# Opening of a fused attention and GEGLU kernel: x and wk loaded in halves, fewer zero matmuls, x transposed in the logits' banks, K chunks side by side, beta and gate_w late

## The chip, the cores and the metric

The kernel runs on one core of a Trainium2 chip. The metric is the device time of one execution in microseconds (us). Five engines work side by side, each with its own instruction queue: TensorE (PE, matmuls; its weight loads are shown as PEld), VectorE (DVE), ScalarE (ACT), GpSimd (POOL) and SyncE (SP, which issues most DMAs). Each takes its instructions in order; where one needs another's result, it waits on a semaphore, and everything behind it on that engine waits too.

## The reference, cut to what matters

x is 2048 rows of 512; the attention has 32 heads of 16 and works in 4 segments of 512 rows, with a memory M, z carried from one to the next; beside it stands a gated feed-forward of width 1792.

```python
g = sigmoid((x * gate_w).sum(-1, keepdims=True))
# A: per segment s
p = softmax(q_s k_s^T * 16**-0.5 + mask);  a_dot = p v_s
a_mem = (phi(q_s) M) / (phi(q_s) z + 1e-6)
o = sigmoid(beta) * a_mem + (1 - sigmoid(beta)) * a_dot
M += phi(k_s)^T v_s;  z += sum(phi(k_s))        # then o @ wo
# B
b = (gelu(x @ w_gate) * (x @ w_up)) @ w_down
return g * a + (1 - g) * b
```

## The kernel before

All tensors live in SBUF for the whole run. x is held transposed (xT, 512 features as 4 blocks `fc` of 128 partitions, 2048 columns), since every projection contracts over features. The weights wq, wk, wv, wga (gate), wup, wdn, wo are loaded whole. G[0..2] hold the feed-forward's activations of a segment; G[1] is lent at the start to the first segment of x (x0) and a block of zeros.

The work is written in program order by hand (a manual schedule), in two parts.

**The opening** is a fixed list:

- `load_inputs` (L118): SP issues in this order x0 (L125), wk, wq, beta, wv, wga (all L120 through `cols`, beta L128), the DMA transpose of x's segment 1 (L123), gate_w (L132), wup, the transposes of segments 2 and 3, wdn, wo.
- `warm_up` (L143): DVE clears the zeros, PE runs 9 matmuls of 128x512 on them.
- `transpose_x0` (L149): for each of the 4 blocks fc, PE transposes 4 tiles of x0 into a bank T of the pool `gen`, and DVE (fc 0, 2, L156) or ACT (fc 1, 3, L158) copies the bank to xT. Each fc has its own bank.
- `setup_consts` (L160): masks, by POOL, and two small reductions on DVE.
- K of segment 0 (`u_k`, L290): three of the four chunks of 128 columns, one after another; each is 4 matmuls (one per fc) into a bank of `gen`, then DVE evicts it to ktb (L299) and multiplies it by two masks into KT (L301). Then four chunks of Q (`u_q`, L239 matmul, L244 eviction by DVE), four row tiles of V (`u_v`, L316, L320), `setup_beta` (L174: ACT's Exp of beta, then three small DVE operations to gh and og), and 14 gate chunks (`u_gate`, L360) that ACT evicts with its Gelu (L366). After the fourth of these DVE takes four absolute maxima (L185).

**The rest** is planned at build time. Streams (K, Q, V, G, U, D, O and so on) hold units of work with costs and due times; a loop over 4 segments, 4 column chunks and 5 groups A to E puts the logits of a group (L519) on PE, their Exp on ACT (L525), the masking on POOL, and fills PE with units of the streams until the Exp should be done. One unit's matmuls go into a bank of `gen` and DVE evicts it; a gate chunk of a later segment is evicted by a copy (L368) and an up chunk by a product (L387).

PSUM has 8 banks: 4 are the logits tile `lg` (pool `plg`, one buffer), 1 is `od`, and `gen` has 3. A matmul that opens a `gen` bank waits until its last user's eviction is done.

Of the kernel before, what the change touches and what calls it, by code (L numbers as in the profile page):

```python
# [13 lines left out]
P = 128  # L14
D = 512
H = 32
# [3 lines left out]
FC = D // P  # L20
NC8 = H // 8
HS = DFF // P
EXP_LIMIT = 80.0
NG = 3
NK = 3
BF = dt.bfloat16
# [18 lines left out]
def kernel(  # L45
# [15 lines left out]
    nc = tc.nc  # L61
    S = A_x.shape[1]
    L = S // NSEG
    KT = L // P
    assert A_x.shape[0] == 1 and A_x.shape[2] == D and L == 512 and KT == 4
    x2 = A_x[0]
# [5 lines left out]
    plg = ctx.enter_context(tc.tile_pool(name="plg", bufs=1, space=bass.MemoryType.PSUM))  # L72
    pod = ctx.enter_context(tc.tile_pool(name="pod", bufs=1, space=bass.MemoryType.PSUM))
    pgen = ctx.enter_context(tc.tile_pool(name="pgen", bufs=3, space=bass.MemoryType.PSUM))

    def const(shape, dtype, name):
        return cpool.tile(shape, dtype, name=name, tag=name)

    xT = const([P, FC, S], BF, "xT")
    wq = const([P, FC, D], BF, "wq")  # L80
    wk = const([P, FC, D], BF, "wk")
    wv = const([P, FC, D], BF, "wv")
    wo = const([P, FC, D], BF, "wo")
    wup = const([P, FC, DFF], BF, "wup")
# [3 lines left out]
    ident = const([P, P], BF, "ident")  # L88
    bm = const([P, 8, 17], BF, "bm")
    eo = const([P, 2], F32, "eo")  # L90
    beta = const([P, H], BF, "beta")
# [8 lines left out]
    phk = const([P, NC8, L], BF, "phk")  # L100
    G = [const([P, HS, L], BF, f"G{i}") for i in range(NG)]
    QT = const([P, NC8, L], BF, "QT")
# [12 lines left out]
    def gen(name):  # L115
        return pgen.tile([P, 512], F32, name=name, tag="gen")

    def load_inputs():  # L118
        def cols(dst, src):
            nc.sync.dma_start(dst[:, :, :], src.rearrange("(fc p) n -> p fc n", p=P))  # L120

        def x_seg(s):
            nc.sync.dma_start_transpose(xT[:, :, s * L:(s + 1) * L], x2[s * L:(s + 1) * L, :])  # L123

        nc.sync.dma_start(x0, x2[0:L, :].rearrange("(k p) d -> p k d", p=P))  # L125
        cols(wk, A_wk)
        cols(wq, A_wq)
        nc.sync.dma_start(beta[:, :], A_beta.rearrange("(o n) -> o n", o=1).to_broadcast((P, H)))  # L128
        cols(wv, A_wv)
        cols(wga, B_w_gate)  # L130
        x_seg(1)
        nc.sync.dma_start(gw[:, :], gate_w.rearrange("(fc p) -> p fc", p=P))  # L132
        cols(wup, B_w_up)
        x_seg(2)
        x_seg(3)
        cols(wdn, B_w_down)
        cols(wo, A_wo)


    x0 = G[1][:, 0:KT, :]  # L140
    zero = G[1][:, KT, :]

    def warm_up():  # L143
        nc.vector.memset(zero, 0.0)
        T = gen("warm")
        for i in range(9):
            nc.tensor.matmul(T[:, :], lhsT=zero[:, 0:P], rhs=zero, start=True, stop=True)

    def transpose_x0():  # L149
        for fc in range(FC):  # L150
            T = pgen.tile([P, 1024], BF, name="x0T", tag="gen")
            for kt in range(KT):
                nc.tensor.transpose(T[:, kt * P:(kt + 1) * P],
                                    x0[:, kt, fc * P:(fc + 1) * P], ident[:, :])
            if fc % 2 == 0:
                nc.vector.tensor_copy(xT[:, fc, 0:L], T[:, 0:512])  # L156
            else:
                nc.scalar.copy(xT[:, fc, 0:L], T[:, 0:512])  # L158

    def setup_consts():  # L160
        nc.gpsimd.memset(bm[:, :, :], 1.0)
# [12 lines left out]
    def setup_beta():  # L174
        eb = wk2.tile([P, H], F32, name="eb", tag="eb")
        nc.scalar.activation(eb[:, :], beta[:, :], AF.Exp, scale=-1.0)
        nc.vector.tensor_scalar_add(eb[:, :], eb[:, :], 1.0)
        nc.vector.reciprocal(gh[:, :], eb[:, :])
        nc.vector.tensor_scalar(out=og[:, :], in0=gh[:, :], scalar1=-1.0, scalar2=1.0,
                                op0=ALU.mult, op1=ALU.add)  # L180
# [3 lines left out]
    def absmax(i, src):  # L184
        nc.vector.tensor_reduce(out=amax[:, i:i + 1], in_=src, axis=mybir.AxisListType.XY,  # L185
                                op=ALU.max, apply_absolute_value=True)
# [10 lines left out]
    def u_bound():  # L197
# [8 lines left out]
        def spread():  # L206
            room_for_bank()
            T = gen("bT")
            for i in range(3):
# [7 lines left out]
        def test():  # L217
# [4 lines left out]
            nc.vector.tensor_scalar(out=safe[:, :], in0=bound[:, 5:6],  # L222
                                    scalar1=float(DH ** 0.5 * D * D), scalar2=EXP_LIMIT,
                                    op0=ALU.mult, op1=ALU.is_le)
# [65 lines left out]
    def u_k(s, c):  # L290
        def f():
            T = gen("kT")
            for fc in range(FC):
                nc.tensor.matmul(T[:, :], lhsT=wk[:, fc, c * P:(c + 1) * P],  # L294
                                 rhs=xT[:, fc, s * L:(s + 1) * L],
                                 start=(fc == 0), stop=(fc == FC - 1))
                if fc < FC - 1:
                    yield MM512
            nc.vector.tensor_copy(ktb[:, c, :], T[:, :])  # L299
            for p in range(2):  # L300
                nc.vector.tensor_scalar(out=KTm[p][:, (NC8 * s + c) % NK, :], in0=ktb[:, c, :],  # L301
                                        scalar1=eo[:, p:p + 1], scalar2=None, op0=ALU.mult)
            return MM512
        return 4 * MM512, EVAC + 0.6, f
# [7 lines left out]
    def u_v(s, kt):  # L312
        def f():
            T = gen("vT")
            for fc in range(FC):
                nc.tensor.matmul(T[:, :], lhsT=xT[:, fc, s * L + kt * P:s * L + (kt + 1) * P],  # L316
                                 rhs=wv[:, fc, :], start=(fc == 0), stop=(fc == FC - 1))
                if fc < FC - 1:
                    yield MM512
            nc.vector.tensor_copy(V[s % 2][:, kt, :, 0:16],  # L320
                                  T[:, :].rearrange("p (h d) -> p h d", h=H))
            return MM512
        return 4 * MM512, EVAC, f
# [32 lines left out]
    def u_gate(s, hs, direct):  # L356
        def f():
            T = gen("gT")
            for fc in range(FC):
                nc.tensor.matmul(T[:, :], lhsT=wga[:, fc, hs * P:(hs + 1) * P],  # L360
                                 rhs=xT[:, fc, s * L:(s + 1) * L],
                                 start=(fc == 0), stop=(fc == FC - 1))
                if fc < FC - 1:
                    yield MM512
            if direct:
                nc.scalar.activation(G[s % NG][:, hs, :], T[:, :], AF.Gelu_apprx_tanh)  # L366
            else:
                nc.vector.tensor_copy(G[s % NG][:, hs, :], T[:, :])  # L368
            return MM512
        return 4 * MM512, EVAC, f  # L370

    def gelu(s):
        for h0 in range(0, HS, 7):
            g = G[s % NG][:, h0:h0 + 7, :]
            nc.scalar.activation(g, g, AF.Gelu_apprx_tanh)  # L375

    def u_up(s, hs):
        def f():
            T = gen("uT")
            for fc in range(FC):  # L380
# [3 lines left out]
                if fc < FC - 1:  # L384
                    yield MM512
            g = G[s % NG][:, hs, :]
            nc.vector.tensor_tensor(out=g, in0=T[:, :], in1=g, op=ALU.mult)  # L387
# [5 lines left out]
    def u_down(s, qt):  # L393
        def f():
            T = gen("dT")
            for hs in range(HS):
                nc.tensor.matmul(T[:, :], lhsT=G[s % NG][:, hs, qt * P:(qt + 1) * P],  # L397
                                 rhs=wdn[:, hs, :], start=(hs == 0), stop=(hs == HS - 1))
# [175 lines left out]

    ctx.enter_context(tc.manual_schedule())
    load_inputs()
    make_identity(nc, ident[:, :])
    warm_up()
    transpose_x0()
    setup_consts()  # L580

# [38 lines left out]
    def room_for_bank():  # L620


        if current:
            current[0][3][0] += 1
            while current and current[0][3][0] > 2:
                step()
# [37 lines left out]
    def run(u):  # L664
        if u[0] == 0.0:
            u[2]()
        else:
            for _ in u[2]():
                pass

    for c in range(NK):
        run(u_k(0, c))
    for c in range(NC8):
        run(u_q(0, c))
    for kt in range(KT):
        run(u_v(0, kt))
    setup_beta()
    done["k", 0], done["q", 0], done["v", 0] = NK, NC8, KT
    for hs in range(HS):
        run(u_gate(0, hs, True))  # L680
        if hs == 3:
            absmax(1, wq[:, :, :])
            absmax(2, wk[:, :, :])
            absmax(0, xT[:, :, 0:L])
        if hs == HS - 3:
            absmax(3, xT[:, :, L:2 * L])
    t_act[0] = t_pe[0] + 1.9

    def u_gelu(s):
# [13 lines left out]
    for i in range(NK, NSEG * NC8):  # L703
        s, c = i // NC8, i % NC8
# [8 lines left out]
    for i in range(NC8, NSEG * NC8):  # L713
        s, c = i // NC8, i % NC8
# [99 lines left out]
    for s in range(NSEG):  # L814
        oT = wk2.tile([P, FC, L], BF, name="oT", tag="oT")
        oTs[s] = oT
        for c in range(NC8):
            for g in "ABCDE":
# [25 lines left out]
                n = 4 * NC8 * 5 - clock[0]  # L844
# [152 lines left out]
```

## Time and profile before

| what | us |
|---|---|
| median of 3 runs | 292.79 (292.26 to 293.21) |
| the profiled execution | 293.84 |
| its span, first to last instruction | 292.0 |
| PE busy | 282.9 (97%) |
| DVE busy | 215.7 (74%) |
| ACT busy | 200.7 (69%) |
| POOL busy | 82.7 (28%) |

How to read it: the page lists busy times, then the chain of waits that ended last, then groups of instructions with the idle time ahead of them and its releaser; a DMA's time is from its issue to its landing. The timeline view lists instructions by time: start, length, engine, line, operation, output and input, count, and in brackets the idle time of the engine before it and what ended it. Neighbouring instructions of one kind stand in one row, so a row's length is from the first's start to the last's end. Matmuls are pipelined: one begins before the one ahead of it has ended.

Landings of the first loads, from issue (page, last part): x0 3.9 us, wk 4.8, wq 9.0, beta 8.8, wv 9.7, wga 13.7, gate_w 3.1, wup 8.7.

### The profile page before, as it was taken

The page shows a single profiled execution, that of the slowest core. Times are in us where ns is not written, and L with a number is a line of the kernel's source. Part 1 is how long each engine was busy: PE and PEld are TensorE (multiplying, and loading weights), DVE is VectorE, ACT ScalarE, POOL GpSimd, SP SyncE. Part 2 cuts the span into 40 slices and gives each one's busy share as a digit, 9 for nine tenths or more (in the row PEclk, how much of TensorE's full clock was granted, in tenths as well). Part 3 has the DMA queues.
Part 4 walks back from the last instruction along what each step waited for, and adds up shares of the span by engine and source line. Part 5 has one row for each costly group of instructions (what it writes and reads, how often), then busy time and mean ns, then how long its engine had stood idle before and what let it go on. Part 6 is the DMA issues. An engine that isn't in the chain of part 4 may idle for free.

```text
span 292.0 us, 6916 instructions
## 1 busy us (share of the span) xinstructions
PE 282.9 (97%) x2960; PEld 138.2 (47%) x2960; DVE 215.7 (74%) x422; ACT 200.7 (69%) x125; POOL 82.7 (28%) x140
## 2 busy tenths in 40 slices
PE   7899999999999999999999999999999999999992
PEld 4344445554444454545444454455544544544451
DVE  1788488777876869987878968988768567785453
ACT  3226877768897776776898785767748968777600
POOL 4000043344204334243410424242323033244300
PEclk9999999999999999999999999999999999999998
DMA  6989940200000000400000001033101000011002
GB/s 214 325 189 251 308 84 3 54 20 2 20 0 2 20 20 18 93 20 20 18 20 18 2 2 36 3 76 34 38 0 38 2 0 20 18 21 38 22 19 79
DMA packets 29444, 15.85 MB, mean 54 GB/s; under 512 B 21984, under 2 KB 28384, under 8 KB 29408
## 3 DMA queue, kind: packets, MB, share of 16 engines
q1 hardware_dynamic: 29408, 15.35, 21.0%
q8 instruction: 25, 0.41, 0.6%
q14 instruction: 11, 0.09, 0.1%
HBM read 8.14 MB, written 2.10 MB: 35 GB/s over the span
## 4 chain that ended last, share of the span: by engine, by line
PE 56%; DVE 3%; issue 0%; DVEq 0%
PE dT L397 14%; PE uT L381 10%; PE od L546 7%; PE gT L360 6%; PE lg L519 6%; PE aT L414 4%; PE kT L294 2%; PE vT L316 2%; PE qT L239 2%; PE mn L496 1%; PE MT L434 1%; DVE ktb L299 0%; DVE G L368 0%; DVE pha L271 0%; DVE o L556 0%
## 5 line engine op out<-in xcount | busy, mean ns | idle before, releaser
L525 ACT ACTIVATE pT<-lg 128x2048 bf16<-128x2048 f32 x80 | 150.1, 1876 | 57.1 <-PE lg L519 46.0
L536 POOL TENSOR_SCALAR_AFFINE_SELECT pT<-pT 128x512 bf16<-128x512 bf16 x128 | 79.5, 639 | 194.1 <-ACT pT L525 192.2
L381 PE MATMUL uT<-xT,wup 128*128 128x512 bf16 x224 | 62.3, 379 | 0.0
L360 PE MATMUL gT<-xT,wga 128*128 128x512 bf16 x224 | 60.2, 379 | 0.6 <-DVE G L368 0.4
L397 PE MATMUL dT<-wdn,G 128*128 128x512 bf16 x224 | 55.2, 379 | 0.2 <-DVE G L387 0.2
L546 PEld LDWEIGHTS <-pT 128*128 128x128 bf16 x1280 | 43.6, 96 | 17.7 <-issue 0.4
L546 PE MATMUL od<-V,pT 128*128 128x17 bf16 x1280 | 43.9, 170 | 0.0
L387 DVE TENSOR_TENSOR G<-uT,G 128x512 bf16<-128x512 f32 x56 | 38.3, 686 | 6.8 <-PE uT L381 6.4
L368 DVE CAST G<-gT 128x512 bf16<-128x512 f32 x42 | 28.8, 685 | 8.0 <-PE gT L360 7.7
L519 PE MATMUL lg<-QT,KT 32*128 32x384 bf16 (+3 forms) x512 | 31.7, 301 | 0.0
L360 PEld LDWEIGHTS <-wga 128*128 128x128 bf16 x224 | 19.7, 97 | 22.8 <-issue 5.5
L397 PEld LDWEIGHTS <-G 128*128 128x128 bf16 x224 | 19.5, 97 | 22.2 <-issue 3.9
L381 PEld LDWEIGHTS <-wup 128*128 128x128 bf16 x224 | 19.2, 97 | 20.8 <-issue 5.0
L402 DVE TENSOR_SCALAR tB<-dT,omg 128x512 bf16<-128x512 f32 x16 | 12.0, 750 | 19.9 <-PE dT L397 19.8
L519 PEld LDWEIGHTS <-KT 32*128 32x128 bf16 x512 | 8.9, 92 | 29.8 <-issue 29.5
L375 ACT ACTIVATE G<-G 128x3584 bf16<-128x3584 bf16 x6 | 18.8, 3182 | 0.0
L239 PE MATMUL qT<-xT,wq 128*128 128x512 bf16 x64 | 17.4, 379 | 1.1 <-DMA wq<-in_A_wq_dram 1.1
L552 DVE RECIPROCAL rden<-od 128x16 f32<-128x16 f32 x32 | 8.2, 256 | 13.7 <-PE od L546 13.4
L294 PE MATMUL kT<-xT,wk 128*128 128x512 bf16 x64 | 17.1, 380 | 0.3 <-DVE xT L156 0.3
L414 PE MATMUL aT<-wo,oT 128*128 128x512 bf16 x64 | 16.4, 379 | 0.5 <-DVE G L368 0.5
L316 PE MATMUL vT<-wv,xT 128*128 128x512 bf16 x64 | 16.4, 380 | 0.0
L366 ACT ACTIVATE G<-gT 128x512 bf16<-128x512 f32 x14 | 8.4, 598 | 9.7 <-PE gT L360 9.7
(81 smaller groups left out, 226.2 us busy)
## 6 DMA issues: line engine op xcount, KB each, us to landing
out_dram<-osb SPq DMA_DIRECT2D x16, 128.0 KB, 1.7
wga<-in_B_w_gate_dram SPq DMA_DIRECT2D x1, 1792.0 KB, 13.7
wup<-in_B_w_up_dram SPq DMA_DIRECT2D x1, 1792.0 KB, 8.7
wdn<-in_B_w_down_dram SPq DMA_DIRECT2D x1, 1792.0 KB, 10.3
G<-in_A_x_dram SPq DMA_DIRECT2D x1, 512.0 KB, 3.9
wk<-in_A_wk_dram SPq DMA_DIRECT2D x1, 512.0 KB, 4.8
wq<-in_A_wq_dram SPq DMA_DIRECT2D x1, 512.0 KB, 9.0
wv<-in_A_wv_dram SPq DMA_DIRECT2D x1, 512.0 KB, 9.7
```

Of the source, the lines that this page charges most:

```text
L239: nc.tensor.matmul(T[:, :], lhsT=wq[:, fc, c * P:(c + 1) * P], rhs=xT[:, fc, s * L:(s + 1) * L], start=(fc == 0), stop=(fc == FC - 1))
L294: nc.tensor.matmul(T[:, :], lhsT=wk[:, fc, c * P:(c + 1) * P], rhs=xT[:, fc, s * L:(s + 1) * L], start=(fc == 0), stop=(fc == FC - 1))
L360: nc.tensor.matmul(T[:, :], lhsT=wga[:, fc, hs * P:(hs + 1) * P], rhs=xT[:, fc, s * L:(s + 1) * L], start=(fc == 0), stop=(fc == FC - 1))
L368: nc.vector.tensor_copy(G[s % NG][:, hs, :], T[:, :])
L381: nc.tensor.matmul(T[:, :], lhsT=wup[:, fc, hs * P:(hs + 1) * P], rhs=xT[:, fc, s * L:(s + 1) * L], start=(fc == 0), stop=(fc == FC - 1))
L387: nc.vector.tensor_tensor(out=g, in0=T[:, :], in1=g, op=ALU.mult)
L397: nc.tensor.matmul(T[:, :], lhsT=G[s % NG][:, hs, qt * P:(qt + 1) * P], rhs=wdn[:, hs, :], start=(hs == 0), stop=(hs == HS - 1))
L414: nc.tensor.matmul(T[:, :], lhsT=oT[:, fc, qt * P:(qt + 1) * P], rhs=wo[:, fc, :], start=(fc == 0), stop=(fc == FC - 1))
L519: nc.tensor.matmul(lg[:, j, off:off + n], lhsT=KTm[pp][32 * j:32 * j + 32, (NC8 * s + c) % NK, kt * P:(kt + 1) * P], rhs=QT[32 * j:32 * j ...
L525: nc.scalar.activation(pT[:, :, :], lg[:, :, :], AF.Exp, scale=DH ** -0.5)
L536: nc.gpsimd.affine_select(out=v, in_=v, pattern=pat, compare_op=ALU.is_ge, fill=0.0, base=0, channel_multiplier=-1)
L546: nc.tensor.matmul(od[:, qq, j, 0:17], lhsT=t[:, j, o:o + P], rhs=V[s % 2][:, kt, 8 * c + 2 * j + p, 0:17], start=(kt == 0), stop=(kt == qq))
```

## The change

- x0 comes in two DMAs: row tiles 2 and 3 issued by ACT, row tiles 0 and 1 by SP. wk comes in two DMAs of two fc blocks each.
- beta moves from its place behind wq, and gate_w from its place ahead of wup, to behind wup.
- 4 zero matmuls instead of 9.
- x0's transposes go into one tile of four banks from the logits' pool, first all fc blocks of row tiles 0 and 1, then those of row tiles 2 and 3; each fc block is copied when its second half is done, by the same engines as before.
- The three K chunks are begun side by side: fc 0 of all three, fc 1 of all three, then fc 2 and 3 of each with its eviction.
- `setup_beta` stands behind the 14 gate chunks instead of behind V.

```diff
-        nc.sync.dma_start(x0, x2[0:L, :].rearrange("(k p) d -> p k d", p=P))
-        cols(wk, A_wk)
+        rows = x2[0:L, :].rearrange("(k p) d -> p k d", p=P)
+        nc.scalar.dma_start(x0[:, 2:4, :], rows[:, 2:4, :])
+        nc.sync.dma_start(x0[:, 0:2, :], rows[:, 0:2, :])
+        wkr = A_wk.rearrange("(fc p) n -> p fc n", p=P)
+        nc.sync.dma_start(wk[:, 0:2, :], wkr[:, 0:2, :])
+        nc.sync.dma_start(wk[:, 2:4, :], wkr[:, 2:4, :])
         cols(wq, A_wq)
-        nc.sync.dma_start(beta[:, :], A_beta.rearrange("(o n) -> o n", o=1).to_broadcast((P, H)))
         cols(wv, A_wv)
         cols(wga, B_w_gate)
         x_seg(1)
+        cols(wup, B_w_up)
         nc.sync.dma_start(gw[:, :], gate_w.rearrange("(fc p) -> p fc", p=P))
-        cols(wup, B_w_up)
+        nc.sync.dma_start(beta[:, :], A_beta.rearrange("(o n) -> o n", o=1).to_broadcast((P, H)))
...
-        for i in range(9):
+        for i in range(ZEROS):
             nc.tensor.matmul(T[:, :], lhsT=zero[:, 0:P], rhs=zero, start=True, stop=True)
...
-        for fc in range(FC):
-            T = pgen.tile([P, 1024], BF, name="x0T", tag="gen")
-            for kt in range(KT):
-                nc.tensor.transpose(T[:, kt * P:(kt + 1) * P],
-                                    x0[:, kt, fc * P:(fc + 1) * P], ident[:, :])
-            if fc % 2 == 0:
-                nc.vector.tensor_copy(xT[:, fc, 0:L], T[:, 0:512])
-            else:
-                nc.scalar.copy(xT[:, fc, 0:L], T[:, 0:512])
+        T = plg.tile([P, FC, 1024], BF, name="x0T", tag="lg")
+        for k0 in (0, 2):
+            for fc in range(FC):
+                for kt in (k0, k0 + 1):
+                    nc.tensor.transpose(T[:, fc, kt * P:(kt + 1) * P],
+                                        x0[:, kt, fc * P:(fc + 1) * P], ident[:, :])
+                if k0 == 2 and fc % 2 == 0:
+                    nc.vector.tensor_copy(xT[:, fc, 0:L], T[:, fc, 0:L])
+                elif k0 == 2:
+                    nc.scalar.copy(xT[:, fc, 0:L], T[:, fc, 0:L])
+
+    def first_k():
+        us_ = [u_k(0, c)[2]() for c in range(NK)]
+        for _ in range(2):
+            for u in us_:
+                next(u)
+        for u in us_:
+            for _ in u:
+                pass
...
-    for c in range(NK):
-        run(u_k(0, c))
+    first_k()
     for c in range(NC8):
         run(u_q(0, c))
     for kt in range(KT):
         run(u_v(0, kt))
-    setup_beta()
...
+    setup_beta()
     t_act[0] = t_pe[0] + 1.9
```

More of the change, by code (lines that the diff above doesn't have):

```diff
@@ L23 @@
 EXP_LIMIT = 80.0
+ZEROS = 4
 NG = 3
```

## The prediction

> **What bounds the kernel now.** I read the page first: PE is busy 97% of the span, and the chain that ended last is PE work almost throughout, so whatever holds PE anywhere is paid at the end. The profiled execution took 293.84 us, a span of 292.0 us and 1.84 us around it; the median shown is 292.79. The change touches the opening and the end of the gate chunks, so next I read the timeline there (start, length, engine, line, what, count, idle time before it and its releaser).
>
> ```profile
> 0.81 1.28 ACT L158 ACT_TABLE_LOAD   x1 [0.81 <-PEq L981]
> ...
> 1.26 4.02 PE L147 MATMUL warm<-G 128*128 128x512 bf16 x9 [1.26 <-DVE G L144]
> ...
> 4.71 0.10 PEld L153 LDWEIGHTS <-G 128*128 128x128 bf16 x1 [0.34 <-DMA G<-in_A_x_dram]
> 5.07 1.69 PE L153 MATMUL x0T<-ident,G 128*128 128x128 bf16 x16
> ...
> 5.74 0.42 DVE L156 COPY xT<-x0T 128x512 bf16<-128x512 bf16 x1 [4.54 <-PE x0T L153]
> 6.17 1.21 ACT L158 COPY xT<-x0T 128x512 bf16<-128x512 bf16 x2 [4.08 <-PE x0T L153]
> ...
> 7.05 2.75 PE L294 MATMUL kT<-xT,wk 128*128 128x512 bf16 x12 [0.29 <-DVE xT L156]
> ...
> 8.11 0.69 DVE L299 CAST ktb<-kT 128x512 bf16<-128x512 f32 x1 [0.98 <-PE kT L294]
> ...
> 9.37 0.68 DVE L299 CAST ktb<-kT 128x512 bf16<-128x512 f32 x1
> ...
> 10.95 3.63 PE L239 MATMUL qT<-xT,wq 128*128 128x512 bf16 x16 [1.15 <-DMA wq<-in_A_wq_dram]
> ...
> 14.41 3.62 PE L316 MATMUL vT<-wv,xT 128*128 128x512 bf16 x16
> ```
>
> See three things. The table load of ACT lies at 0.81, under the wait for x. PE waits 0.29 us for copies and 1.15 us for wq. From 14.41, the first V matmul, PE runs without a hole: I measure the opening by when V starts.
>
> The tile view of G and wk (shortest/median/longest ns) shows the clock:
>
> ```profile
> L153 PEld LDWEIGHTS <-G x16: 98/151/151, 4.7 to 6.5; 128*128 128x128 bf16 x16
> ...
> L147 PE MATMUL warm<-G x9: 607/634/634, 1.3 to 4.6; 128*128 128x512 bf16 x9
> ```
> ```profile
> L294 PE MATMUL kT<-xT,wk x12: 376/379/379, 7.1 to 9.4; 128*128 128x512 bf16 x12
> ```
>
> A full matmul takes 634 ns before and 379 ns after some moment, and the loads 151 and 98. The zeros start 0.427 us apart (weight loads at 2.08, 2.51, 2.94), the K matmuls 0.216 us ((2.75 - 0.38) / 11), the transposes 0.107. By the tile view of short stretches the loads are of 151 ns up to 6.2 and of 98 from 6.4: PE worked about 5.1 us without a pause (from 1.26) before it ran at full speed. (The clock column says 1.00 from 0; no record lies before the first turn, so these rows carry it.)
>
> The end of the gate chunks:
>
> ```profile
> 30.77 1.28 ACT L525 ACT_TABLE_LOAD   x1
> ...
> 31.45 0.69 DVE L368 CAST G<-gT 128x512 bf16<-128x512 f32 x1 [3.23 <-PE gT L360]
> ...
> 32.06 1.88 ACT L525 ACTIVATE pT<-lg 128x2048 bf16<-128x2048 f32 x1
> 32.11 1.89 PE L360 MATMUL gT<-xT,wga 128*128 128x512 bf16 x8
> ```
>
> DVE copies the next gate chunk at 31.45 while ACT loads its table until 32.05.
>
> **The opening, step by step.** The changed kernel's instruction order holds more than the diff says. All of x0T is now one tile, and its copies and the second half's transposes wait for each other in turn: PE's transposes of fc 1 wait for DVE's copy of fc 0, those of fc 2 for ACT's copy of fc 1, those of fc 3 for DVE's copy of fc 2; ACT's first copy waits for DVE's, and ACT stands at that wait ahead of its table load, which so leaves 0.81.
>
> 1. x lands. Now its load is waited for until 4.71. The windows view has 82 GB/s in 2.0 to 2.5, 365 in 3.0 to 3.5: the start is slow, and two queues can shorten it, not the rest. Between 4.0 and 4.7; I take 4.4. Eight transposes of the first half: 0.05 + 8 x 0.107 = 0.9, so fc 0's second half starts at 5.3.
> 2. The chain. Two transposes take 0.107 + 0.314 (tile view), DVE starts 0.04 later (5.70 to 5.74) and copies 0.425: +0.89. ACT wakes (0.05), loads 1.28 and copies 0.59: +2.81. PE wakes (0.06), fc 2: 0.42, DVE 0.04 + 0.43, PE 0.06: fc 3 starts at +3.81; after its two transposes K starts at +4.02, since its first six matmuls need only fc 0 and 1, and ACT's last copy (0.59) lies under them. K starts at 9.3, not 7.05: **+2.25**. Bounds: +1.7 (x at 4.0 with 0.2 less of wakes), +2.6 (x at 4.7). Without the load in the chain it would be +0.95.
> 3. The clock. Four zeros end at about 3.0; then PE pauses for 1.4 us, works 0.9, and has only four pairs of transposes up to 9.3. Now it took 5.1 us of unbroken work. So K runs at 0.427. Its first chunk's last matmul is the eighth: 7 x 0.427 + 0.63 + 0.04, DVE starts to evict at K + 3.66. From there DVE sets the pace: 1.26 us a chunk (8.11, 9.37), the fourth Q chunk needs the bank that the first QT copy frees, 3 x 1.26 + 0.69 + 0.05 = 4.52 later, and V starts 4 x 0.216 after: K + 9.04. Now V starts 7.36 after K. **+1.7.** Bounds: at full speed from the start the eviction begins at K + 1.93 and V at K + 7.31, that is 0; slow to the end of the first Q chunk V comes at K + 9.4, +2.0. I stay near the upper end, as the row nearest to it (5.1 us) is.
>
> The Trainium skill, "TensorE: Matmul & The Clock Gate", Part 1, says that the gate opens after one busy window of some 3.4 us, and that the windows run free of the kernel's start. By it the gate could open 3.4 to 6.8 us after K starts, which leaves +1.7 to +2.0; the 5.1 us here agree.
>
> What costs nothing: the fifth to ninth zeros lay under the wait for x. wq is issued one issue (0.5 us) later, behind the second half of wk; it landed at 10.9 (1.86 + 9.0), and Q now starts at 14.4: 3.5 us of cover. This hides, too, that without beta's packets it may land earlier; the 1.15 us are thus no gain. The side by side order saves the 0.29, counted in 2. gw and beta go behind wup on SP's queue, issued by 18.7, ahead of the two x transposes: gw took 3.1 us and wup 8.7, so both are there by 28, and are needed from 32. The transposes stand behind the same number of issues as before, less beta's.
>
> **The end of the gate chunks.** beta's Exp moves behind the last gate activation and the table load, so it runs at 32.06 to 32.29 (0.23; times of now, all shifted). DVE has its three small ops ahead of the gate copy, and they wait for that Exp: the copy that stood at 31.45 waits until 32.33 + 0.69 (18.67 to 19.36 now) = 33.02. Behind it stand the up product and the next gate copies. PE has three banks: the third gate chunk after it, second half of the x8 at 32.11, starts at 32.98 and needs the bank of that copy, free at 33.02 + 0.69 + 0.05 = 33.76: **+0.78**. The bounds are 0 (a later hole takes it up) and 1.0 (if the next chunk is held as well). The 0.23 that ACT's first pT is late hides beneath: the next logits stand at 34.15 and move to 34.9, the Exp ends at 34.2.
>
> **Sum**: 2.25 + 1.7 + 0.75 = +4.7 us on a PE that has no later hole to absorb it: 298.5 for the profiled execution, which stands 1.05 above the median; the median goes to **297.5**.
>
> **Rivals.**
> - The clock turns early (short pauses count as work): K at full speed. 2.25 + 0.75: 295.8. For it: only about half of the time up to K is idle. Against: nine zeros needed 5.1 us. 14%.
> - The late beta is absorbed: 2.25 + 1.7: 296.7. For it: DVE idles 3.23 us before 31.45. Against: the Exp itself comes after that. 12%.
> - Not slower: the copies don't hold each other, and ACT's load stays at its start. Then K starts at 5.3 + 0.9 = 6.2, and with the clock turned at 6.4 as now V starts 7.31 later, at 13.5: -0.9, +0.75 of beta: 292.7. It decides if K starts before 7.0; the waits in the order speak against it. 4%.
> - The table load costs more than its row when it is waited for. Twice 1.28 on the chain: 298.8. Against: now 30.77 to 32.06 is 1.29 with nothing after it. 6%. The Trainium skill, "ScalarE: Activation LUTs", What ACT_TABLE_LOAD costs, has 1.28 us for the load and 1.38 for a drain on a switch of set; by it the sum would be 1.4 more. The row here shows no drain.
>
> Forecast 64%. The range reaches over all but the not-slower case: 295.4 (early clock, x at 4.0) to 298.9. Faster by over 0.3% 0.03, within 0.3% (0.9 us, about what a measurement of this kernel tells from no change) 0.03, slower 0.94.
>
> **What would show it.** After: ACT's table load between the first DVE copy and the first ACT copy; second-half transposes in pairs with holes; K from about 9.3 with 634 ns matmuls; V at about 18.4; DVE idle until ACT's Exp, and right behind it a PE hole of 0.8 us on a gate chunk. Wrong if K starts near 7, if K's matmuls are of 379 ns, or if V is at 14.

## The result, and the profile after

The changed kernel takes **299.25 us** (median of 6 runs, 298.92 to 299.41) against 292.94 (median of 6 runs of the kernel before, 292.26 to 293.21): ratio 1.0217, 95% interval 1.0203 to 1.0231. It is 6.3 us slower, where 4.7 were forecast. Its profiled execution took 299.41 us, a span of 297.5 and 1.91 around it.

The timeline of the changed kernel's opening (columns as in the prediction: start, length, engine, line, what, count, idle time before and its releaser; the transposes are now L160, DVE's copy L163, ACT's L165, K L311, Q L256, V L333):

```profile
4.50 1.25 PE L160 MATMUL x0T<-ident,G 128*128 128x128 bf16 x10 [1.35 <-DMA G<-in_A_x_dram]
...
5.78 0.42 DVE L163 COPY xT<-x0T 128x512 bf16<-128x512 bf16 x1 [4.58 <-PE x0T L160]
...
6.26 0.37 PE L160 MATMUL x0T<-ident,G 128*128 128x128 bf16 x2 [0.52 <-DVE xT L163]
...
6.29 1.28 ACT L165 ACT_TABLE_LOAD   x1 [6.29 <-DVE xT L163]
7.58 0.59 ACT L165 COPY xT<-x0T 128x512 bf16<-128x512 bf16 x1
8.22 0.37 PE L160 MATMUL x0T<-ident,G 128*128 128x128 bf16 x2 [1.59 <-ACT xT L165]
...
9.18 0.37 PE L160 MATMUL x0T<-ident,G 128*128 128x128 bf16 x2 [0.59 <-DVE xT L163]
...
9.35 5.08 PE L311 MATMUL kT<-xT,wk 128*128 128x512 bf16 x12
...
14.26 3.01 PE L256 MATMUL qT<-xT,wq 128*128 128x512 bf16 x12
...
17.50 1.02 PE L256 MATMUL qT<-xT,wq 128*128 128x512 bf16 x4 [0.23 <-DVE QT L261]
...
18.36 3.62 PE L333 MATMUL vT<-wv,xT 128*128 128x512 bf16 x15
```

Read the last bracket of each line as a chain. The second halves come in pairs, each after the copy of the block before, and the copies after the pairs. The table load, which stood at 0.81 before, now starts at 6.29 behind DVE's copy, and PE sits idle 1.59 us until ACT's copy is through. K starts at 9.35 instead of 7.05, and its 12 matmuls take 5.08 us instead of 2.75. V starts at 18.36 instead of 14.41.

The timeline where the gate chunks end (the late Exp is L193, DVE's three small ops L194 to L196, its gate copy L385, the gate matmuls L377):

```profile
34.71 1.28 ACT L193 ACT_TABLE_LOAD   x1
...
36.01 0.23 ACT L193 ACTIVATE eb<-beta 128x32 f32<-128x32 bf16 x1
...
36.27 0.18 DVE L194 TENSOR_SCALAR eb<-eb 128x32 f32<-128x32 f32 x1 [4.79 <-ACT eb L193]
...
36.96 0.68 DVE L385 CAST G<-gT 128x512 bf16<-128x512 f32 x1
...
37.70 1.02 PE L377 MATMUL gT<-xT,wga 128*128 128x512 bf16 x4 [0.61 <-DVE G L385]
```

DVE idles 4.79 us until the Exp that stands behind the table load, and its gate copy then holds a bank that PE wants: a hole of 0.61 us. Matched instruction by instruction, PE runs 3.95 us later than before from V on, 4.72 later from the matmul at 37.70 on, and 4.73 later at the last weight load. No later hole takes anything back.

The end of the span, in the tile view of out_dram from 280 us on, the kernel before and then the changed one (shortest/median/longest, first and last start of an issue; then the time from issue to landing):

```profile
L423 SPq DMA_DIRECT2D out_dram<-osb x5: 332/332/332, 280.1 to 287.7; - x5
...
DMA to landing us min/median/max: 1.7/1.7/2.7
```
```profile
L440 SPq DMA_DIRECT2D out_dram<-osb x5: 332/332/333, 284.8 to 292.4; - x5
...
DMA to landing us min/median/max: 1.7/1.7/3.0
```

The longest landing is that of the last store. By the landing records it lands at 290.38 before, 1.60 us ahead of the end of the span (292.0), and at 295.47 after, 2.02 ahead of the end (297.5). So 4.73 us come from PE, 0.35 from a store that took longer to land, 0.42 from what comes after the landing, 0.06 from the time around the span, and the last 0.01 from between PE's end and the store's issue: 5.57 in all (299.41 - 293.84). That is 0.9 more than the 4.7 forecast for this execution. The medians are a further 0.74 apart, which the experiments explain.

### The profile page after: what moved, and what is told of

Same layout as the page of the kernel before. It is cut to its first block, busy times and chain, and to the rows that moved or that the text cites. A ratio compares the mean times of both kernels' runs of the same rounds, so it can differ in the third digit from the quotient of the medians.

```text
span 297.5 us, 6862 instructions
## 1 busy us (share of the span) xinstructions
PE 279.1 (94%) x2905; PEld 138.1 (46%) x2955; DVE 215.2 (72%) x422; ACT 200.6 (67%) x125; POOL 83.0 (28%) x140
## 3 DMA queue, kind: packets, MB, share of 16 engines
HBM read 8.14 MB, written 2.10 MB: 34 GB/s over the span
## 4 chain that ended last, share of the span: by engine, by line
PE 54%; DVE 3%; issue 1%; DVEq 0%
PE dT L414 13%; PE uT L398 10%; PE od L563 7%; PE gT L377 6%; PE lg L536 6%; PE aT L431 4%; PE kT L311 2%; PE vT L333 2%; PE qT L256 2%; PE mn L513 1%; PE MT L451 1%; DVE ktb L316 0%; DVE G L385 0%; DVE pha L288 0%; DVE o L573 0%
## 5 line engine op out<-in xcount | busy, mean ns | idle before, releaser
L398 PE MATMUL uT<-xT,wup 128*128 128x512 bf16 x207 | 59.1, 379 | 1.4 <-issue 0.8
L377 PE MATMUL gT<-xT,wga 128*128 128x512 bf16 x212 | 57.0, 379 | 1.6 <-DVE G L385 1.0
L414 PE MATMUL dT<-wdn,G 128*128 128x512 bf16 x212 | 53.2, 379 | 1.1 <-issue 0.3
L385 DVE CAST G<-gT 128x512 bf16<-128x512 f32 x42 | 28.7, 684 | 4.5 <-PE gT L377 4.4
L377 PEld LDWEIGHTS <-wga 128*128 128x128 bf16 x224 | 19.7, 97 | 23.5 <-issue 6.4
L311 PE MATMUL kT<-xT,wk 128*128 128x512 bf16 x63 | 19.2, 423 | 0.2 <-DVE rden L570 0.2
L256 PE MATMUL qT<-xT,wq 128*128 128x512 bf16 x58 | 16.4, 379 | 0.6 <-DVE QT L261 0.2
L333 PE MATMUL vT<-wv,xT 128*128 128x512 bf16 x63 | 16.4, 380 | 0.1
```

Source lines behind the costliest of these rows:

```text
L256: nc.tensor.matmul(T[:, :], lhsT=wq[:, fc, c * P:(c + 1) * P], rhs=xT[:, fc, s * L:(s + 1) * L], start=(fc == 0), stop=(fc == FC - 1))
L398: nc.tensor.matmul(T[:, :], lhsT=wup[:, fc, hs * P:(hs + 1) * P], rhs=xT[:, fc, s * L:(s + 1) * L], start=(fc == 0), stop=(fc == FC - 1))
```

## The experiments

All times are medians in us; the kernel before was timed on the same chip in each group: 292.51 (7 runs) for the shared tile, the table load, nine zeros alone and beta alone, 292.68 (20 runs) for zeros and tiles together, the repeated profile, the halves and beta on the kernel before, 292.85 (17 runs) for K side by side and the last version. In the changed kernel's own group it was 292.94, so a difference between the changed kernel's median and a median below is good to about 0.4 us.

"The clock rose" means that the profile's records of the granted TensorE clock go to 1.0, "it fell" that they go to 0.5.

### The shared tile

The changed kernel, with four x0T tiles of a bank each from two other pools:

```diff
-        T = plg.tile([P, FC, 1024], BF, name="x0T", tag="lg")
+        T = [pgen.tile([P, 1024], BF, name="x0T", tag="gen") if fc < 3 else
+             pod.tile([P, 1024], BF, name="x0T", tag="od") for fc in range(FC)]
...
```

> The changed kernel with a separate bank for each block of x0T, so that copies and transposes do not wait for each other and ACT's table load goes back to its start. Theory (the turn-by-turn chain with the table load in it costs 3 us): K starts at about 6.3 instead of 9.35, still slow, V at 15.4 instead of 18.36; time 299.25 - 2.9 = 296.3 us. Rival (the halves of x land late or PE is held by something else): K stays at 9 or later, 299 us.

Measured: 295.86 (294.96 to 296.07, 4 runs), ratio 1.0098 (1.0062 to 1.0133). Its timeline:

```profile
1.31 1.28 ACT L166 ACT_TABLE_LOAD   x1 [1.31 <-PEq L998]
...
4.65 1.89 PE L161 MATMUL x0T<-ident,G 128*128 128x128 bf16 x16 [1.50 <-DMA G<-in_A_x_dram]
...
6.41 4.32 PE L312 MATMUL kT<-xT,wk 128*128 128x512 bf16 x12
```

The 16 transposes run in one piece, the table load lies under the wait for x again, and K starts at 6.41, 2.94 earlier. The order of the loads, the halves and the number of zeros are the same: the chain comes from the one tile. The whole time is 3.4 us below the changed kernel's. The matmuls of K are still slow at first (4.32 us for 12; the clock rose at 9.62).

### The table load inside the chain

The changed kernel, with one tiny ACT copy early on (one added instruction that nothing uses), so that the load is done before x is there:

```diff
         nc.vector.memset(zero, 0.0)
+        nc.scalar.copy(hm[:, 0:1], zero[:, 0:1])
```

> The changed kernel with one tiny copy on ACT at the start, which brings the table load forward; the turn-by-turn waits stay. Theory (the load lies on the chain at its full length): K at 8.1, V at 17.1, time 299.25 - 1.3 = 297.95 us. Rival (the load was hidden by the other steps): 299.2 us.

Measured: 298.14 (298.03 to 298.31, 4 runs), ratio 1.0184 (1.0153 to 1.0215), so 1.1 less than the changed kernel (1.0 by the two ratios). From the first DVE copy to K it is 2.65 us instead of 3.57: the load cost 0.92 there, and the rest of its 1.28 lay over fc 1's transposes, which ACT had to wait for in any case. The load is about a third of the chain's cost.

### Nine zeros again

```diff
-ZEROS = 4
+ZEROS = 9
```

> The changed kernel with nine zero matmuls again. Theory (four zeros leave the clock low for all of K): the zeros end at 5.2, so the chain begins 0.65 us later and K starts at 9.95, but at full speed with matmuls of 379 ns; V comes 7.3 us after K at 17.25 instead of 18.36: 298.1 us. Rival (the holes of the chain bring the low clock back, or the zeros do not set it): V at 19.0, 299.9 us.

Measured: 299.10 (298.54 to 299.67, 4 runs), ratio 1.0218 (1.0183 to 1.0254): nothing gained. The windows view of its opening (stretch, length, busy time and count of PE, PEld, DVE, ACT and POOL, granted clock, DMA share, GB/s):

```profile
4.00:8.00 4.00, 1.80 (x18) 1.09 (x16) 0.42 (x1) 1.87 (x2) 0.00 (x1) 0.96 0.97 308
8.00:12.00 4.00, 3.41 (x12) 1.29 (x11) 0.56 (x3) 1.87 (x2) 0.00 (x0) 0.50 1.05 411
12.00:16.00 4.00, 4.00 (x14) 1.56 (x13) 3.24 (x8) 0.00 (x0) 0.00 (x0) 0.69 1.24 271
```

The clock was up early (by its records at 4.26, after 3.0 us of zeros), and the pauses of the chain brought it down again at 7.67: from 8 to 12 it was granted 0.50, and it rose again at 14.50, so K was as slow as with four zeros. The theory that four zeros alone leave the clock low fell: with this chain, five more zeros ahead of x gain nothing, since the pauses undo them.

### Zeros and tiles together

The changed kernel with both edits, nine zeros and separate tiles:

```diff
-ZEROS = 4
+ZEROS = 9
...
-        T = plg.tile([P, FC, 1024], BF, name="x0T", tag="lg")
+        T = [pgen.tile([P, 1024], BF, name="x0T", tag="gen") if fc < 3 else
+             pod.tile([P, 1024], BF, name="x0T", tag="od") for fc in range(FC)]
...
```

> The changed kernel with separate banks and nine zeros. Theory (the low clock through K comes of the pauses, four zeros and the chain together, so with both undone PE works without a pause from 1.26 and K runs with matmuls of 379 ns from about 6.9): V at 14.2, and with the late beta (0.77) and the end (0.42) still in, 295.0 us or up to 0.5 below. Rival (the clock depends on something else): K slow again, V at 15.9, 296.8 us.

Measured: 294.28 (293.92 to 294.98, 5 runs), ratio 1.0054 (1.0035 to 1.0073). The timeline of its opening:

```profile
5.99 2.87 PE L312 MATMUL kT<-xT,wk 128*128 128x512 bf16 x12 [0.18 <-DVE xT L164]
...
8.03 0.69 DVE L317 CAST ktb<-kT 128x512 bf16<-128x512 f32 x1 [1.63 <-PE kT L312]
...
10.03 1.02 PE L257 MATMUL qT<-xT,wq 128*128 128x512 bf16 x4 [0.23 <-DVE ktb L317]
...
11.28 1.02 PE L257 MATMUL qT<-xT,wq 128*128 128x512 bf16 x4 [0.23 <-DVE ktb L317]
...
12.53 1.02 PE L257 MATMUL qT<-xT,wq 128*128 128x512 bf16 x4 [0.23 <-DVE QT L262]
```

The clock rose at 4.42 and K runs at full speed: 2.87 us for its 12 matmuls, against 4.32 with separate tiles and four zeros, and the time is 1.6 below that run's (294.28 against 295.86). So the zeros do count once the chain is gone; either the pauses or the missing zeros were enough to keep K slow. K also starts some 0.9 us earlier than in the kernel before (5.99), and still the kernel is 1.6 slower than that. A part of this is a new cost: Q's chunks come every 1.25 us, each behind a hole of 0.23 for a DVE eviction, and V starts 7.40 us after K (13.39). That is DVE's pace, not PE's.

### Beta alone

The changed kernel with beta, gate_w and `setup_beta` at their old places:

```diff
         cols(wq, A_wq)
+        nc.sync.dma_start(beta[:, :], A_beta.rearrange("(o n) -> o n", o=1).to_broadcast((P, H)))
...
+    setup_beta()
     done["k", 0], done["q", 0], done["v", 0] = NK, NC8, KT
...
-    setup_beta()
     t_act[0] = t_pe[0] + 1.9
```

> The changed kernel with beta's and gate_w's loads and beta's operations at their old places. Theory (the late beta holds DVE ahead of a gate copy and PE for 0.77 us): the hole near 37 us is gone and the time is 299.25 - 0.78 = 298.5 us; the opening does not change, since Q starts at 14.3, after any landing of wq. Rival (a later hole would have taken it up): 299.25 us.

Measured: 298.31 (297.82 to 298.73, 4 runs), ratio 1.0190 (1.0156 to 1.0224). The hole at the gate chunk is gone, and PE runs 0.95 us earlier than in the changed kernel from there on; 0.18 of that it already had at V, since its clock rose earlier (12.35 against 14.04). What is left is 0.77, the same as in the changed kernel's trace.

### The kernel before, profiled again

No edit.

> The kernel before, unchanged, profiled once more. Theory (the profiled execution of the prediction was longer than the median because wq landed late in it, which the changed kernel does not feel): PE's hole ahead of the first Q matmul is 0.4 us or less instead of 1.15, and the span is 291.2 or less instead of 292.0. Rival (the longer time lies elsewhere, or is what the profile itself costs): the hole stays at 1.0 to 1.2 us, or is small with a span of 292.

Measured: 292.83 (one run), span 290.9. Its timeline:

```profile
6.89 2.75 PE L294 MATMUL kT<-xT,wk 128*128 128x512 bf16 x12 [0.28 <-DVE xT L156]
...
9.47 2.75 PE L239 MATMUL qT<-xT,wq 128*128 128x512 bf16 x12
...
12.45 1.02 PE L239 MATMUL qT<-xT,wq 128*128 128x512 bf16 x4 [0.22 <-DVE QT L244]
...
13.31 3.62 PE L316 MATMUL vT<-wv,xT 128*128 128x512 bf16 x16
```

The hole of 1.15 us ahead of Q, which the prediction's execution shows, isn't there: Q follows K at once, and V starts 6.42 us after K, not 7.36. V is 1.10 earlier, and the span 1.1 shorter (290.9 against 292.0). In the prediction's execution wq landed at 10.90, in this one at 8.14; the landing records show that 15 of its 16 shares were there by 8.33 and one came 2.6 us later. So the profile that the prediction was made from had a late transfer in it, which the median doesn't have.

### K side by side, alone

The kernel before, with `first_k` of the change:

```diff
-    for c in range(NK):
-        run(u_k(0, c))
+    first_k()
```

> The kernel before with its three K chunks begun side by side, nothing else. Theory (the evictions of the three chunks come in a bunch and DVE then sets Q's pace; it costs as much as V comes later after K: 7.40 us in the repaired banks with nine zeros, 6.42 in the second profile of before): V at K + 7.3 to 7.4, 0.9 us slower than before, 293.6 us. Rival (as the prediction had it, the order only saves the wait for the copies): 292.4 us.

Measured: 293.87 (293.57 to 294.07, 6 runs), ratio 1.0038 (1.0024 to 1.0051). Its timeline:

```profile
6.45 2.83 PE L304 MATMUL kT<-xT,wk 128*128 128x512 bf16 x12 [0.16 <-DVE eo L178]
...
8.45 0.69 DVE L309 CAST ktb<-kT 128x512 bf16<-128x512 f32 x1 [2.02 <-PE kT L304]
...
10.45 1.02 PE L249 MATMUL qT<-xT,wq 128*128 128x512 bf16 x4 [0.23 <-DVE ktb L309]
```

K begins 0.44 earlier than in the repeated profile of before (a part of this is the clock, which rose at 4.31 here and at 6.04 there: the 16 transposes take 1.30 us instead of 1.53). But the first eviction comes 2.00 after K's start instead of 1.06, since no chunk is complete until the eighth matmul. All three banks are then full, and Q waits for DVE's evictions one by one. V comes 7.36 after K instead of 6.42, a loss of 0.94; the medians lose 1.0. The prediction's own value for this kernel, no loss, fell.

### The halves, and beta, on the kernel before

The kernel before with x and wk in halves as in the change, nothing else:

```diff
-        nc.sync.dma_start(x0, x2[0:L, :].rearrange("(k p) d -> p k d", p=P))
-        cols(wk, A_wk)
...
+        nc.scalar.dma_start(x0[:, 2:4, :], rows[:, 2:4, :])
+        nc.sync.dma_start(x0[:, 0:2, :], rows[:, 0:2, :])
...
+        nc.sync.dma_start(wk[:, 0:2, :], wkr[:, 0:2, :])
+        nc.sync.dma_start(wk[:, 2:4, :], wkr[:, 2:4, :])
...
```

> The kernel before with x0 and wk in halves on two queues, nothing else. Theory (the halves bring nothing, and two more DMAs move the last store's semaphore from the last to the second of the eight that SP waits for at the end, six waits of 0.07 us behind it): V at 14.4 to 14.9, last landing to end of span 2.02 instead of 1.61 us, time 292.9 to 293.6 us. Rival (two queues bring x in sooner): V at 14.0 or earlier and 292.2 us; rival for the end (the 0.42 us are landing noise): 1.6 us from the last landing to the end.

Measured: 293.01 (292.64 to 293.51, 10 runs), ratio 1.0009 (0.9995 to 1.0023). The halves landed at 4.55 and 4.88; the whole of x landed at 4.67 to 4.95 in the four profiles that load it in one DMA. So two queues bring the first half a little earlier, and the whole of x no earlier. The Trainium skill, "DMA: Bandwidth & Descriptors", has in "Issuing engines are not separate DMA queues" that the queues of two engines feed the same 16 DMA engines; these landings agree. With two more DMAs, the span ends 2.02 after the last landing, as in the changed kernel.

The kernel before with beta and gate_w loaded behind wup, the Exp one step behind the first pT and DVE's three ops two steps later, so that nothing urgent stands behind a wait:

```diff
...
-        nc.scalar.activation(eb[:, :], beta[:, :], AF.Exp, scale=-1.0)
...
+        def f_exp():
+            nc.scalar.activation(eb[:, :], beta[:, :], AF.Exp, scale=-1.0)
...
+        later(1, f_exp)
+        later(3, f_gates)
...
-    setup_beta()
...
+    setup_beta()
```

> The kernel before with beta and gate_w loaded behind wup, beta's Exp behind the first pT on ACT and its three DVE operations three groups in, so that neither waits. Theory (beta's small packets delay wq): wq lands by 8, K, Q and V follow each other without a hole and V starts at 13.5; against a median of 292.6 a gain of 0.2 to 0.9: 292.0 us. Rival (wq's delay has another cause): the hole before Q stays as in the kernel before, 292.6 us.

Measured: 292.67 (292.00 to 293.37, 10 runs), ratio 1.0000 (0.9984 to 1.0015). wq landed at 8.12, no earlier than with beta's packets beside it (8.14). So beta's load isn't what makes wq late, and moving beta is worth nothing; the expected gain didn't come. Done like this it costs nothing either: in its profile PE is 0.50 us ahead of the repeated profile of before at K, where the clock rose at 5.00 instead of 6.04, and still 0.48 ahead at the last weight load. The span is no shorter (290.8 against 290.9), since the last store took 0.44 us longer to land. What made one share of wq late in one execution, and how often that happens, stays open: in all the other profiles wq took 5.6 to 6.7 us from issue to landing, against the 9.0 there.

### A version without the losses

x in halves, separate tiles, eight zeros, K in turn, wk whole, beta late as just shown, and x segments 2 and 3 in one transposing DMA so that there are 56 DMAs again:

```diff
...
-        x_seg(2)
-        x_seg(3)
+        nc.sync.dma_start_transpose(xT[:, :, 2 * L:4 * L], x2[2 * L:4 * L, :])
...
-    first_k()
+    for c in range(NK):
+        run(u_k(0, c))
...
```

> What is left of the change when its costs are taken out: x in halves on two queues, transposes by halves into four separate banks, eight zeros, K chunks in turn, wk whole, beta and gate_w late with beta's operations after the first groups, and x's last two segments in one transpose so that there are 56 DMAs as before. Theory (each cost is what the other runs showed): K at 6.0 to 6.3, V 6.4 later at 12.4 to 12.7 against 13.3, the end 1.6 us after the last landing: 291.8 us, 0.8 below before. Rival (the clock or wq holds K or Q in most executions): 292.7 us, no gain.

Measured: 292.69 (292.43 to 293.11, 12 runs), ratio 0.9994 (0.9983 to 1.0004). K starts at 6.43 instead of 6.89, but the clock rose at 7.21 in its profile, so K's 12 matmuls took 3.12 instead of 2.75 and V came at 13.22 (13.31 in the repeated profile of before). The expected 0.8 us didn't come: mended, the change is worth nothing that can be measured. In the one profile, what PE gains by starting earlier it spends at the low clock; whether that is so in most executions isn't shown.

## Why the prediction was right in direction and short in size

**1. x lands (4.4).** Right for the first half: SP's half lands at 4.45, ACT's at 4.78, and the first transpose starts at 4.50. That "two queues can shorten it" isn't borne out for x as a whole: with the halves alone it lands no earlier.

**2. The chain (+2.25).** Right: K starts at 9.35, forecast 9.3. With separate tiles and the same loads and zeros K starts 2.94 earlier, so the cause is shown. "Without the load" it was to be 1.3 less; without it the chain was 0.92 shorter, since a part of the load was hidden.

**3. The clock (+1.7).** The size was right: V comes 9.01 after K, forecast 9.04. The reason behind it, "it took 5.1 us of unbroken work", was not: 5.1 us is what one execution took. With nine zeros ahead of the chain the clock rose after 3.0 us, and fell again in the pauses. The last section has what decides. The rival "the clock turns early (short pauses count as work)" lost on that: ahead of the window in which the clock was won, PE worked at most 1.9 of 3.41 us in any. A part of the close hit is luck: the clock rose at 14.04, after K's first chunk was complete; with beta at its old place it rose at 12.35, and V came 8.72 after K.

**4. What costs nothing.** The cover of wq held: it landed at 9.06, and Q started at 14.26. Here, though, lies the first of the two steps that failed: "The side by side order saves the 0.29, counted in 2". Alone it costs 1.0 us. The price was in reach of the prediction's own working, which has V 7.31 after K at full clock; it was set against 7.36, the distance in an execution in which wq was late, and so came out as 0. Against the 6.42 of the repeated profile it is +0.9.

**5. Beta (+0.78).** Right: +0.77, with the wait chain as written.

**The sum.** For the profiled execution 4.7 were forecast on PE, and 4.73 came. That the two agree so well is luck: the late wq, 1.10 us in that execution, hid the order of K, 0.98 us, which the sum had left out. "298.5 for the profiled execution, which stands 1.05 above the median; the median goes to 297.5" was the second step that failed: the 1.05 was the late wq. The changed kernel covers wq, so it has no such surplus (its profiled execution is 0.16 above its median). The two steps are one error seen from two sides, and together account for 0.89 of the 1.75 that the forecast of 297.5 lacks. Of the rest, 0.42 is a term that the prediction didn't have, the end of the span, 0.35 is the last store's landing, which varies between 2.66 and 3.16 us over the profiles here, and 0.1 the small differences above.

Against the repeated profile of before the terms are:

| term | how | us |
|---|---|---|
| later start of K: the chain, less what x's first half gains | 9.35 - 6.89 | 2.46 |
| low clock through K | 9.01 - 7.40 (side by side at full speed) | 1.61 |
| K side by side | 7.40 - 6.42 | 0.98 |
| late beta | 4.72 - 3.95 | 0.77 |
| more waits at the end | 2.02 - 1.60 | 0.42 |
| sum | | 6.24 |

The medians are 6.31 apart. The spans of these two executions are 6.62 apart; the remaining 0.38 is nearly all the last store's landing, 0.35 longer in the one than in the other.

**The rivals.** "The late beta is absorbed" fell (0.77 stays to the end). "Not slower" fell, since the copies and transposes do hold each other. "The load costs more than its row" gave nearly the measured time (298.8) by a mechanism that isn't there: from the load's start to the copy behind it are 1.29 us (6.29 to 7.58), with no drain behind the load.

## What to carry to other kernels

A multi-bank tile that several engines write and read in parts can chain them as if it were one buffer; look at the instruction order for waits that the diff doesn't show, and at what stands on an engine behind such a wait, a table load among it. Profile the kernel before more than once: a term that is charged against a hole is only as good as the hole, and here one late transfer of 1.1 us hid the price of an order that fills all banks before it empties one. Work that warms the clock must reach without pauses up to the work that needs it.

## What the runs showed of the hardware

- **The clock's steps keep a raster of 3.413 us.** With nine zeros in the changed kernel it rose at 4.26, fell at 7.67 and rose at 14.50: once and twice that length. Over the kernels it first rose anywhere between 4.26 and 14.04, and at 4.31 to 6.38 in the six profiles with nine zeros and no chain behind them, so the start of the raster differs from one execution to the next. The Trainium skill, "TensorE: Matmul & The Clock Gate", Part 1, has windows of 3413 ns that run free of the kernel; the records agree. If windows of 3.413 us are counted back from the first rise, PE was busy for 3.00 to 3.41 us in the last one ahead of it, in all twelve profiles, and for 2.54 us or less in every earlier one (1.62 and 1.82 in the changed kernel; 2.54 in the version without the losses, whose eight zeros began 0.9 us into their window). With nine zeros in the changed kernel a window with 1.41 us of PE work, most of it transposes, brought the clock down, and the next one, with 2.62 us, left it there. So it takes one nearly full window, not 5.1 us; how long that is from the first zero depends on where the raster lies.
- **Two more DMAs put off the end of the span.** In the five profiles with 56 DMAs the span ends 1.60 us after the last landing, in the seven with 58 it ends 2.02 after it. The DMAs count on eight semaphores in turn, and SP waits for these one after the other at the end: with 56 the last store's is the last of the eight, with 58 the second, and six waits of 0.07 us follow.
- **One of the 16 shares of a DMA can be 2.6 us behind the others** (wq: 8.33 and 10.90), in one execution and not in the next.
